# A retention-plus-Fourier-mixer kernel: the last batch pinned on every engine, its normalisation cut into separate pieces

## The chip, the cores and the metric

The kernel runs on one core of one Trainium2 chip. The metric is the device time of one execution in microseconds (us), lower is better. Three runs of the kernel before are given: 245.81, 246.08 and 246.43 us, median 246.08 us. One more execution was profiled; all durations in the prediction are from that one.

## The reference: what is computed

Two parts follow each other. The first is a recurrent retention layer with 4 batches, 8 heads, 768 steps and head size 64; the second takes its output as a tensor x of 4 x 768 x 512.

```python
for t in range(S):                       # retention, per batch and head
    state = gamma * state + outer(k[t], v[t])
    y[t] = scale * q[t] @ state
x = y, heads side by side                # (4, 768, 512)
u = x + real(fft(fft(x, axis=1), axis=2))
un = (u - mean(u)) / sqrt(var(u) + 1e-6) # over the 512 columns
out = u + relu(un @ w_ch1) @ w_ch2       # 512 -> 2048 -> 512
```

All inputs and the output are float32; the kernel multiplies in float16 and adds up in float32.

## The kernel before

Each batch is worked as 6 row blocks of 128 rows (index kb, 0 to 5). Four groups of work follow each other for a batch b: the retention (`attn_steps`, heads in pairs), the Fourier mixing of a row block (`s2_unit`: four matmuls L838, two copies on ScalarE L840/L841, two adds on VectorE L845/L848, two adds of x on GpSimd L875/L877), its normalisation (`norm_unit`, L895/L896 and after), its transposition (`unT_unit`; in the last batch a DMA transpose issued by SP, L938), and the two large matrix products. The matmuls of the products of batch b are the backbone, and the retention and the mixing of batch b+1 are sprinkled between them. `emit` sorts all units by a due time (b plus a fraction) and calls them in that order; the tile framework then schedules instructions on each engine by its own estimate, unless a manual dependency holds them. `pin` adds such dependencies: each instruction behind the one that stood before it on its engine. Before the change `pin` holds all engines only for the first batch's opening; up to time 1.0 it holds GpSimd; after that nothing.

The last batch (b = 3) differs from the others. Its products are made per pair of row blocks, p = 0, 1, 2. `h3_unit(p, n)`, n = 0 to 7, makes hidden blocks n and n+8 for the 256 rows of pair p: eight matmuls of 256 columns into one PSUM bank, tag `pm`, three banks in all (`ps_pm`). The bank is emptied with a ReLU into `ht16` by ScalarE (L1044) or by VectorE (L1046), as `H3_ACT` says: before the change VectorE has n = 2, ScalarE the other seven. Behind n = 3 and n = 7 VectorE makes four sums of `ht16` blocks each (L1063, called hsum here). `p3_unit(p, n)` then makes the seven products of a Strassen-like scheme (56 matmuls, L1103; 72 in pair 2, where two products go in column halves), and VectorE (L1096) and GpSimd (L1126) add them up; `wsum_unit` (L1024) has prepared sums of the second weight. The products of p = 0 follow in the order 1, 4, 2, 5, 6, 7, 3, and each row block's store goes out through SP (L1099).

Row blocks 0 to 2 of the last batch are mixed and normalised while the products of batch 2 still run; blocks 3, 4 and 5 while the last batch's own products run, at the due times `MIX3`: one tuple for each block, with times for mixing, `norm_unit`, `scaled_unit` and `unT_unit`. Pair p = 0 needs blocks 0 and 1 transposed, p = 1 blocks 2 and 3, p = 2 blocks 4 and 5. For the last batch the normalisation has these steps: statistics on VectorE (L895, L896), root on ScalarE (L898), reciprocal on VectorE (L912), a product mean times reciprocal on VectorE (L913), and on ScalarE the scaled rows `un` in float16 (L916). `un` has two buffers.

Batch 0's output rows are stored by `ch_unit` (L1004), one DMA of 128 x 512 float32 for each row block, on SP's queue, among the loads of later batches (L170) and the DMA transposes.

Of the kernel before, what the change touches and what calls it, by code (L numbers as in the profile page):

```python
# [11 lines left out]
AF = mybir.ActivationFunctionType  # L12
ALU = mybir.AluOpType
# [5 lines left out]
P = 128  # L19
B, H, S, D = 4, 8, 768, 64  # L20
DM = 512
# [15 lines left out]
LD0, LD1 = (0.172, 0.226), (-0.370, 0.140)  # L37
HT0 = (0.655, 0.675, 0.673, 0.628)
NPE = 2
MIX3 = ((0.005, 0.035, 0.070, 0.105), (0.190, 0.310, 0.325, 0.350), (0.355, 0.395, 0.420, 0.470))  # L40
WS = (0.7, 1.05)
H3_ACT = (0, 1, 3, 4, 5, 6, 7)
PROD = ((1, 4, 2, 5, 6, 7, 3), (1, 4, 6, 7, 5, 2, 3))
HS_AT = {3: (0, 4), 7: (4, 8)}
ACT_ROWS = ((2, 5, 6, 7, 8, 9, 10, 14), (0, 3, 6, 7, 9, 10, 11, 12, 14, 15))
# [3 lines left out]
def kernel(  # L49
# [9 lines left out]
    nc = tc.nc  # L59
# [36 lines left out]
    epsT = const.tile([P, 1], f32, tag="epsT")  # L96
# [10 lines left out]
    mark = [0]  # L107

    def pin(engines=None):
        ins = tc.nc.cur_bb.bb.instructions  # L110
        for n in range(mark[0], len(ins)):
            x = ins[n]
            e = str(x.engine)
            if engines is not None and not any(g in e for g in engines):
                continue
            if e in tails:
                tc.add_manual_dep(x, tails[e],
                                  mybir.DependencyInfo(mybir.DependencyClass.NoSync,
                                                       mybir.DependencyReason.DATA),
                                  reason="pinned order")  # L120
            tails[e] = x.name
        mark[0] = len(ins)
# [86 lines left out]
    for h in range(H):  # L209
# [6 lines left out]
                            op0=ALU.mult)  # L216
# [119 lines left out]
    for j in range(2):  # L336
        x = const.tile([P, NCH, 2, XW], f16, tag=f"x16_{j}", name=f"x16_{j}")
        xts.append(x)
        qz = const.tile([P, 2, NCH, P], f16, tag=f"q16z_{j}", name=f"q16z_{j}")
        qzs.append(qz)  # L340
        qt = const.tile([P, 2, NCH, P], f16, tag=f"qTz_{j}", name=f"qTz_{j}")
        qts.append(qt)
        t = const.tile([P, 257], f32, tag=f"qn_{j}", name=f"qn_{j}", padded_shape=[P, 260])
        nc.gpsimd.memset(t[:, 0:257:256], 0.0)
        qns.append(t)

    hid, nhid = xts[1][:, 0, 0, 0:P], xts[1][:, 0, 1, 0:P]
# [449 lines left out]
    lb = {}  # L797
# [85 lines left out]
    def norm_unit(b, kb):  # L883
        def run():
            u, stats = lb[b]["u"], lb[b]["st"]
            bst = stt.tile([P, 6], f32, tag=f"bst{kb % 3}", name="bst")
            un = up.tile([P, 2, 257], f16, tag="un16", name="un16").rearrange(
                "p a b -> p (a b)")[:, 0:DM]
            if b == 0 and kb < 3:
                for c0, c1 in (((0, 256), (256, DM)) if kb == 0 else ((0, DM),)):  # L890
                    una = nc.scalar.activation(un[:, c0:c1], u[:, kb, c0:c1], AF.Identity,
                                               bias=fd[0]["mu"][:, kb:kb + 1], scale=-1.0)
                lb[b]["bst", kb] = bst
            else:
                nc.vector.bn_stats(bst, u[:, kb, :])  # L895
                nc.vector.bn_aggr(stats[:, kb, 0:2], bst)  # L896
                if b == B - 1:
                    nc.scalar.activation(stats[:, kb, 2:3], stats[:, kb, 1:2], AF.Sqrt,  # L898
                                         bias=epsT, scale=1.0)
                    lb[b]["un", kb] = un  # L900
                    return
                una = nc.scalar.activation(un, u[:, kb, :], AF.Identity,  # L902
                                           bias=stats[:, kb, 0:1], scale=-1.0)
            lb[b]["un", kb] = un
            if b == 0 and kb == 2:
                lb[0]["una"] = una
        return run

    def scaled_unit(kb):
        def run():  # L910
            u, stats = lb[B - 1]["u"], lb[B - 1]["st"]
            nc.vector.reciprocal(out=stats[:, kb, 3:4], in_=stats[:, kb, 2:3])  # L912
            nc.vector.scalar_tensor_tensor(out=stats[:, kb, 2:3], in0=stats[:, kb, 0:1],  # L913
                                           scalar=-1.0, in1=stats[:, kb, 3:4], op0=ALU.mult,
                                           op1=ALU.mult)
            nc.scalar.activation(lb[B - 1]["un", kb], u[:, kb, :], AF.Identity,  # L916
                                 bias=stats[:, kb, 2:3], scale=stats[:, kb, 3:4])
        return run

    def rstd_unit(b, rt):  # L920
# [13 lines left out]
    def unT_unit(b, kb):  # L934
        def run():
            un, unT = lb[b].pop(("un", kb)), lb[b]["unT"]
            if b > 1 or b and kb >= 3:
                nc.sync.dma_start_transpose(unT[:, :, kb * P:(kb + 1) * P], un)  # L938
                return
            pst = ps_g.tile([P, 4, P], f16, tag="g", name="pst", padded_shape=[P, 8, P])  # L940
            for cb in range(4):
                nc.tensor.transpose(pst[:, cb, :], un[:, cb * P:(cb + 1) * P], ident16)
            if b == 0 and kb == 0:
                nc.scalar.copy(unT[:, 0:2, 0:P], pst[:, 0:2])
                nc.scalar.copy(unT[:, 2:4, 0:P], pst[:, 2:4])
            elif (kb % 2 == 0) != (b == 0 and kb < 3):
                nc.vector.tensor_copy(unT[:, :, kb * P:(kb + 1) * P], pst)
            else:
                nc.scalar.copy(unT[:, :, kb * P:(kb + 1) * P], pst)
        return run  # L950
# [39 lines left out]
    def ch_unit(b, rt, rb3, part):  # L990
        def run():
            rb = rt * 3 + rb3
            if part == 0:
                psc_of[0] = ps_pm.tile([P, DM], f32, tag="pm", name="psc")
            psc = psc_of[0]
            for fb in range(4 * part, 4 * part + 4):
                nc.tensor.matmul(psc, ht16[:, fb, rb3 * P:(rb3 + 1) * P], w216[:, fb, :],  # L997
                                 start=(fb == 0), stop=(fb == NFB - 1))
            if part == 3:
                ob = obp.tile([P, DM], f32, tag="ob", name="ob")  # L1000
                nc.vector.scalar_tensor_tensor(out=ob, in0=psc, scalar=lb[b]["st"][:, rb, 3:4],  # L1001
                                               in1=lb[b]["u"][:, rb, :], op0=ALU.mult,
                                               op1=ALU.add)
                nc.sync.dma_start(out[b, rb * P:(rb + 1) * P, :], ob)  # L1004
        return run

    def wsum_unit(j, hi):
# [58 lines left out]
    def p3_unit(p, n):  # L1066
        def run():
# [4 lines left out]
            end = p == 2  # L1072
# [40 lines left out]
            if n == 1:  # L1113
                nc.scalar.copy(w, ps)
            elif n == 2:
                add(o11, ps, u11)
                if end:
                    store(r0, 0, 256, o11)
            elif n == 4:
                add(u21, ps, u21)  # L1120
            elif n == 6:
                add(w, ps, w)
                if end:
                    add(u22, u22, w)
                for x in (u21, u12) if end else (u22, u21, u12):
                    nc.gpsimd.tensor_tensor(out=x, in0=x, in1=w, op=ALU.add)  # L1126
            elif n == 7:
                add(u22 if end else o22, ps, u22)
                add(o21, ps, u21)
                if end:  # L1130
                    store(r1, 0, 256, o21)
                else:
                    store(r1, 0, DM, o1)
# [105 lines left out]
    def mix_units(b, kbs):  # L1239
        s2s = [s2_unit(b, kb) for kb in kbs]  # L1240
        if b == B - 1:
            s2s = [u for kb, s2 in zip(kbs, s2s) for u in (s2, norm_unit(b, kb), scaled_unit(kb))]
        return s2s, [unT_unit(b, kb) for kb in kbs]

    def emit(streams):
        ev = []
        for si, (units, t0, t1) in enumerate(streams):
            for i, u in enumerate(units):
                ev.append((t0 + (t1 - t0) * (i + 1.0) / len(units), si, i, u))
        ev.sort(key=lambda e: e[:3])  # L1250
        for e in ev:
            e[3]()
            if e[0] < 1.0:
                behind()
                pin(None if e[0] < 0.05 else ["Pool", "GpSimd"])

    pin()
    for u in first_units():
# [7 lines left out]
    for b in range(B):  # L1266
# [19 lines left out]
        if b < B - 1:  # L1286
            s2s, unTs = mix_units(b, [3, 4, 5])
            dm = DM0 if b == 0 else DM1
            streams += [(s2s, b + dm[0], b + dm[1]), (unTs, b + dm[2], b + dm[3])]
        else:  # L1290
            for kb, due in zip((3, 4, 5), MIX3):
                streams += [([f], b + t, b + t) for t, f in zip(due, (
                    s2_unit(b, kb), norm_unit(b, kb), scaled_unit(kb), unT_unit(b, kb)))]
        if b + 1 < B:
            steps = attn_steps(b + 1)
            if b == 0:
# [51 lines left out]
```

## Time and profile before

| | us |
|---|---|
| median of three runs | 246.08 (245.81 to 246.43) |
| profiled execution, its own time | 245.54 |
| its span, first to last instruction | 243.8 |
| time around the span | 1.74 |
| TensorE busy in the span | 232.4 |
| VectorE / ScalarE / GpSimd busy | 191.1 / 130.9 / 87.2 |

In the profile PE is TensorE's matmuls, PEld its weight loads, DVE is VectorE, ACT ScalarE, POOL GpSimd, SP SyncE. A line number is that of the kernel before. "Idle before <- X" says that an engine sat idle and that X released it. Two instructions that follow each other on VectorE overlap a little: the next one starts up to 0.09 us before the end shown of the first. The granted TensorE clock was 0.999.

### The profile page before, as it was taken

The numbers are of one execution on the slowest core, as the hardware profiler recorded it, in microseconds if no ns is written. First come the engines' busy times: TensorE is split into PE (matmuls) and PEld (weight loads), VectorE is DVE, ScalarE is ACT, GpSimd is POOL, SyncE is SP. The second block draws the span as 40 slices with busy tenths as digits, with TensorE's granted clock in tenths as the row PEclk, the third lists the DMA queues.
The fourth block names the chain that finished last, engine by engine and source line by source line (L and its number), as shares of the span: only waits on it lengthen the run. The fifth ranks groups of instructions, "written<-read, shape, count | busy, mean of one in ns | idle before, by whom it ended". The sixth has DMA issues, their size and how long they took to land.

```text
span 243.8 us, 5673 instructions
## 1 busy us (share of the span) xinstructions
PE 232.4 (95%) x2160; PEld 156.3 (64%) x2160; DVE 191.1 (78%) x478; ACT 130.9 (54%) x286; POOL 87.2 (36%) x154
## 2 busy tenths in 40 slices
PE   6997899999999998999999999999999999989994
PEld 2454668956776655665567546565667469878883
DVE  8999957897897788996886778899996735775463
ACT  8798669588775434751247414741247527353340
POOL 6666601466600057690000545670002310430302
PEclk9999999999999999999999999999999999999999
DMA  8999999799999477999999467796200231031202
GB/s 174 255 261 143 197 197 205 175 249 246 282 222 225 74 170 167 196 191 133 263 270 216 106 127 207 141 116 145 87 2 1 45 126 46 3 109 24 86 3 86
DMA packets 99498, 36.41 MB, mean 149 GB/s; under 512 B 89872, under 2 KB 96656, under 8 KB 99472
## 3 DMA queue, kind: packets, MB, share of 16 engines
q1 hardware_dynamic: 95104, 31.79, 62.5%
q0 software_dynamic: 4224, 4.19, 10.7%
q8 instruction: 17, 0.28, 0.5%
q14 instruction: 9, 0.07, 0.1%
q10 hardware_dynamic: 144, 0.07, 0.1%
HBM read 27.26 MB, written 6.29 MB: 138 GB/s over the span
## 4 chain that ended last, share of the span: by engine, by line
PE 77%; DVE 6%; ACT 5%; SPq 4%; DMA 3%; issue 2%; POOL 1%; ACTq 0%; POOLq 0%
PE psc L997 25%; PE psh L958 19%; PE psc L1103 8%; PE psh L1039 7%; SPq L170 4%; PE wkA L605 3%; DMA q<-in_q_dram 3%; PE psh L975 3%; PE ps L741 3%; PE wkY L659 2%; PE pq L838 2%; PE wkY L655 1%; PE tq L561 1%; PE wkK L624 1%; ACT g L748 1%
## 5 line engine op out<-in xcount | busy, mean ns | idle before, releaser
L997 PE MATMUL psc<-w,ht 128*128 128x512 f16 x288 | 68.2, 379 | 0.0
L958 PE MATMUL psh<-unT,w 128*128 128x384 f16 x320 | 59.7, 326 | 0.0
L875 POOL TENSOR_TENSOR u<-u,x 128x256 f32<-128x256 f32 x21 | 13.4, 640 | 104.6 <-DVE u L845 95.2
L997 PEld LDWEIGHTS <-ht 128*128 128x128 f16 x288 | 27.2, 98 | 26.1 <-issue 0.2
L958 PEld LDWEIGHTS <-w 128*128 128x128 f16 x320 | 29.9, 98 | 15.8 <-issue 0.6
L962 ACT ACTIVATE ht<-psh 128x384 f16<-128x384 f32 x46 | 22.3, 490 | 23.6 <-PE psh L958 23.4
L608 DVE TENSOR_TENSOR atm<-wkA,maskp 128x512 f16<-128x512 f32 x36 | 23.8, 684 | 1.0 <-PE wkA L605 1.0
L1039 PE MATMUL psh<-unT,w 128*128 128x256 f16 x192 | 21.6, 272 | 0.6 <-DVE ht L1046 0.6
L1039 PEld LDWEIGHTS <-w 128*128 128x128 f16 x192 | 18.7, 98 | 2.9 <-issue 0.8
L964 DVE TENSOR_SCALAR ht<-psh 128x384 f16<-128x384 f32 x34 | 18.6, 549 | 1.8 <-PE psh L958 1.7
L895 DVE BATCH_NORM_STATS2 bst<-u 128x6 f32<-128x512 f32 x21 | 14.6, 695 | 6.6 <-POOL u L877 5.9
L634 DVE SCALAR_TENSOR_TENSOR s<-s,gk,wkK 128x128 f16<-128x128 f16 x48 | 16.5, 343 | 3.0 <-ACT s L630 2.2
L1001 DVE SCALAR_TENSOR_TENSOR ob<-psc,stats,u 128x512 f32<-128x512 f32 x18 | 13.4, 746 | 6.5 <-PE psc L997 6.5
L1044 ACT ACTIVATE ht<-psh 128x512 f16<-128x512 f32 x21 | 12.2, 594 | 10.2 <-PE psh L1039 10.1
L667 ACT ACTIVATE x<-wkY,gexp 128x384 f16<-128x384 f32 x24 | 12.8, 582 | 8.0 <-PE wkY L659 8.0
L902 ACT ACTIVATE un<-u,stats 128x512 f16<-128x512 f32 x15 | 10.8, 722 | 11.0 <-DVE stats L896 7.7
L156 PE MATMUL wps<-ht 128*128 128x512 f16 x40 | 13.5, 443 | 2.2 <-POOL ht L207 2.2
L388 POOL TENSOR_SCALAR kd<-k,gexp 128x384 f16<-128x384 f32 x24 | 13.9, 590 | 3.8 <-DMA k<-in_k_dram 3.8
L877 POOL TENSOR_TENSOR u<-u,x 128x256 f32<-128x256 f32 x21 | 13.3, 635 | 3.0 <-DVE stats L896 1.2
L605 PE MATMUL wkA<-qTz,kT 128*128 128x256 f16 x72 | 13.4, 273 | 0.1
L1126 POOL TENSOR_TENSOR u<-u,ws 128x256 f32<-128x256 f32 x8 | 5.8, 756 | 21.0 <-DVE ws L1096 18.9
L975 PE MATMUL psh<-unT,w 128*128 128x128 f16 x192 | 11.5, 219 | 0.1
(189 smaller groups left out, 424.0 us busy)
## 6 DMA issues: line engine op xcount, KB each, us to landing
q<-in_q_dram SPq DMA_DIRECT2D x16, 384.0 KB, 6.2
k<-in_k_dram SPq DMA_DIRECT2D x16, 384.0 KB, 5.5
v<-in_v_dram SPq DMA_DIRECT2D x16, 384.0 KB, 6.1
out_dram<-ob SPq DMA_DIRECT2D x22, 256.0 KB, 2.5
w<-in_moe_w_ch_dram POOLq DMA_DIRECT2D x8, 512.0 KB, 10.9
out_dram<-ob SPq DMA_DIRECT2D x3, 128.0 KB, 1.7
unT<-un SPq DMA_TRANSPOSE x15, 2.5
qTz<-q16z SPq DMA_TRANSPOSE x8, 3.9
```

Of the source, the lines that this page charges most:

```text
L388: kc = nc.gpsimd.tensor_scalar(out=kd[:, :, h2, :], in0=k32[:, h2], scalar1=gkd[:, h0 + h2:h0 + h2 + 1], scalar2=1.0, op0=ALU.mult, op1=AL ...
L605: mm = nc.tensor.matmul(wk[:, c2], st["kT"][:, c, :], st["qT"][:, :, c, :], start=True, stop=True)
L608: nc.vector.tensor_tensor(out=st["atm"][:, 2 * part:2 * part + 2], in0=wk, in1=maskp[:, PAIR_ORDER[i]].unsqueeze(1).to_broadcast([P, 2, 2, ...
L634: nc.vector.scalar_tensor_tensor(out=s16[:, c], in0=s16[:, c - 1], scalar=gk2[:, hp:hp + 1], in1=wk[:, c - c0], op0=ALU.mult, op1=ALU.add)
L895: nc.vector.bn_stats(bst, u[:, kb, :])
L958: nc.tensor.matmul(psh, w116[:, cb, fb * P:(fb + 1) * P], unT[:, cb, rt * 384:(rt + 1) * 384], start=(cb == 0), stop=(cb == 3))
L962: nc.scalar.activation(ht16[:, fb, :], psh, AF.Relu, bias=0.0, scale=-1.0)
L964: nc.vector.tensor_scalar(out=ht16[:, fb, :], in0=psh, scalar1=-1.0, scalar2=0.0, op0=ALU.mult, op1=ALU.max)
L975: mm = nc.tensor.matmul(psh[:, f], w116[:, cb, fb * P:(fb + 1) * P], unT[:, cb, kb * P:(kb + 1) * P], start=(cb == 0), stop=(cb == 3))
L997: nc.tensor.matmul(psc, ht16[:, fb, rb3 * P:(rb3 + 1) * P], w216[:, fb, :], start=(fb == 0), stop=(fb == NFB - 1))
L1039: nc.tensor.matmul(psh[:, t], w116[:, cb, fb * P:(fb + 1) * P], unT[:, cb, p * 256:(p + 1) * 256], start=(cb == 0), stop=(cb == 3))
L1103: nc.tensor.matmul(ps[:, c0:c1], lh(f), rh(f)[:, c0:c1], start=first and f == 0, stop=last and f == 7, skip_group_check=True)
```

## The change

- `emit` calls `pin()` for every event later than time 3, so the last batch's instructions keep the order in which they are written on all engines; the mark from which `pin` works is moved at each event.
- The last batch's normalisation has a piece more and a smaller one: `root_unit` (the root alone on ScalarE) is separate from `norm_unit`, with a due time of its own in `MIX3`, and `scaled_unit` makes `un` in one VectorE instruction, (u - mean) * reciprocal, in place of the small product on VectorE and the large one on ScalarE. All due times in `MIX3` are new.
- VectorE empties unit n = 4 of each pair in place of n = 2 (`H3_ACT`).
- The last batch's weight sums are due earlier (`WS`).
- Batch 0's stores are two DMAs of 256 columns for each row block.
- On GpSimd, two adds of the same operand for pairs 0 and 1 (u21 and u22) become one of 128 x 512 with the operand repeated; two small memsets at the start are gone.

```diff
-MIX3 = ((0.005, 0.035, 0.070, 0.105), (0.190, 0.310, 0.325, 0.350), (0.355, 0.395, 0.420, 0.470))
-WS = (0.7, 1.05)
-H3_ACT = (0, 1, 3, 4, 5, 6, 7)
+MIX3 = ((0.005, 0.085, 0.110, 0.125, 0.150), (0.190, 0.290, 0.310, 0.325, 0.350),
+        (0.345, 0.415, 0.435, 0.460, 0.500))
+WS = (0.6, 0.97)
+H3_ACT = (0, 1, 2, 3, 5, 6, 7)
...
-        nc.gpsimd.memset(t[:, 0:257:256], 0.0)
...
-                    nc.scalar.activation(stats[:, kb, 2:3], stats[:, kb, 1:2], AF.Sqrt,
-                                         bias=epsT, scale=1.0)
                     lb[b]["un", kb] = un
                     return
...
+    def root_unit(kb):
+        def run():
+            stats = lb[B - 1]["st"]
+            nc.scalar.activation(stats[:, kb, 2:3], stats[:, kb, 1:2], AF.Sqrt, bias=epsT,
+                                 scale=1.0)
+        return run
...
             nc.vector.reciprocal(out=stats[:, kb, 3:4], in_=stats[:, kb, 2:3])
-            nc.vector.scalar_tensor_tensor(out=stats[:, kb, 2:3], in0=stats[:, kb, 0:1],
-                                           scalar=-1.0, in1=stats[:, kb, 3:4], op0=ALU.mult,
-                                           op1=ALU.mult)
-            nc.scalar.activation(lb[B - 1]["un", kb], u[:, kb, :], AF.Identity,
-                                 bias=stats[:, kb, 2:3], scale=stats[:, kb, 3:4])
+            nc.vector.tensor_scalar(out=lb[B - 1]["un", kb], in0=u[:, kb, :],
+                                    scalar1=stats[:, kb, 0:1], scalar2=stats[:, kb, 3:4],
+                                    op0=ALU.subtract, op1=ALU.mult)
...
-                nc.sync.dma_start(out[b, rb * P:(rb + 1) * P, :], ob)
+                for c0, c1 in ((0, 256), (256, DM)) if b == 0 else ((0, DM),):
+                    nc.sync.dma_start(out[b, rb * P:(rb + 1) * P, c0:c1], ob[:, c0:c1])
...
                 if end:
                     add(u22, u22, w)
-                for x in (u21, u12) if end else (u22, u21, u12):
-                    nc.gpsimd.tensor_tensor(out=x, in0=x, in1=w, op=ALU.add)
+                    nc.gpsimd.tensor_tensor(out=u21, in0=u21, in1=w, op=ALU.add)
+                else:
+                    x = u[:, r1].rearrange("p (t m) -> p t m", t=2)
+                    nc.gpsimd.tensor_tensor(out=x, in0=x, in1=w.unsqueeze(1).to_broadcast(
+                        [P, 2, 256]), op=ALU.add)
+                nc.gpsimd.tensor_tensor(out=u12, in0=u12, in1=w, op=ALU.add)
...
             if e[0] < 1.0:
                 behind()
                 pin(None if e[0] < 0.05 else ["Pool", "GpSimd"])
+            elif e[0] > B - 1:
+                pin()
+            mark[0] = len(tc.nc.cur_bb.bb.instructions)
```

## The prediction

> **What bounds the kernel now.** I read the page first, then the busy times by stage, then the waits of TensorE, then the chain of work in the last batch. The page:
>
> ```profile
> span 243.8 us, 5673 instructions
> PE 232.4 (95%) x2160; PEld 156.3 (64%) x2160; DVE 191.1 (78%) x478; ACT 130.9 (54%) x286; POOL 87.2 (36%) x154
> ```
>
> TensorE's matmuls fill 95% of the span; the rest of that share can hide anywhere, so the stages matter. Columns: stage, its length, busy time by engine.
>
> ```profile
> 41.00:96.00 55.00, 54.09 (x554) 36.71 (x552) 45.80 (x117) 34.84 (x69) 21.72 (x34) 1.00 0.95 201
> 96.00:148.00 52.00, 52.00 (x413) 31.57 (x411) 42.08 (x99) 22.13 (x52) 18.83 (x32) 1.00 1.00 188
> 148.00:199.30 51.30, 51.00 (x406) 30.45 (x404) 41.98 (x104) 23.30 (x56) 15.99 (x27) 1.00 0.43 95
> 199.30:213.00 13.70, 13.70 (x133) 12.32 (x131) 9.36 (x27) 7.21 (x16) 3.43 (x6) 1.00 0.10 30
> 213.00:227.00 14.00, 13.38 (x123) 11.60 (x121) 8.66 (x23) 5.83 (x13) 3.60 (x6) 1.00 0.22 58
> 227.00:240.40 13.40, 13.34 (x137) 11.76 (x134) 7.83 (x22) 4.55 (x8) 2.64 (x4) 1.00 0.15 55
> ```
>
> The last three lines are the pairs p = 0, 1, 2 of the last batch, the only stage whose order the change pins. TensorE idles 0.00, 0.62 and 0.06 us there. Of the waits of this stage, only one has PE in front, and the chain shows what stands behind it:
>
> ```profile
> PE psh L1039 <- DVE ht L1046: 0.6, 1, 0.6
> ```
> ```profile
> 213.00 0.89 PE psh L1039 x8
> ...
> 213.97 0.61 ACT ht L1044
> 214.58 0.05 issue
> 214.63 0.49 DVE u L845
> 215.12 0.07 issue
> 215.19 0.64 POOL u L875
> 215.82 0.60 POOL u L877
> 216.43 0.02 issue
> 216.45 0.70 DVE bst L895
> 217.15 0.02 issue
> 217.18 0.18 DVE stats L896
> 217.36 0.58 DVE ht L1046
> 217.95 0.04 issue
> 217.99 2.78 PE psh L1039 x24
> ```
>
> In pair 1 VectorE's emptying of unit n = 2 stands in its queue behind row block 5's statistics, which wait for GpSimd. Unit n = 5 needs the bank of n = 2, so TensorE stops from 217.37 to 217.99. That is the only stall that this change can take away, and **0.62 us is the size of the prize**.
>
> **The change, part by part.**
>
> *TensorE's work.* The built programs (an order with its waits, no times) have the same TensorE stream instruction by instruction. What differs is which of the three banks each unit of the last batch takes and whom it waits for: up to batch 2 nothing, then units n = 3 to 7 of all pairs wait for ScalarE alone. The allocator no longer gives n = 5 or n = 7 the bank that VectorE empties late (n = 4's): n = 5 waits for n = 2 (ScalarE), n = 7 for n = 5 (ScalarE). Only the first product waits for VectorE's n = 4, at its fifth weight load.
>
> *Unit n = 2 moves to ScalarE, n = 4 to VectorE.* In pair 1 ScalarE empties n = 2 as soon as it is made, beside matmuls: the stall goes, **-0.62**. What is late next? ScalarE's eight commands per pair: a bank's unit takes 8 matmuls at 0.109 us (64 in 6.99), the emptying 0.60, so ScalarE keeps up. The tight place is n = 7 behind n = 5. From the last start of n = 5 to the first of n = 7 are nine starts, 0.98 us. Needed: 0.27 (one matmul) + 0.04 to 0.09 (lag of ScalarE behind the matmuls: n = 0 ended at 213.89 and L1044 began at 213.97) + 0.60 + 0.05 (217.94 to 217.99) = 0.96 to 1.01. So 0 to 0.03 for a pair; I take 0.02 each, **+0.06**.
>
> *VectorE's four sums now stand ahead of n = 4.* They need n = 3, which ScalarE ends 2.5 us before the next use; from 203.60 to 205.15 they took 1.55, n = 4 then 0.66: ready at 205.75 in pair 0. The first product's fifth weight load comes at about 206.84 (206.50 + 4 x 0.109, less 0.1): slack 1.1. Pair 2 the same, 0.8. No cost; were the cover gone, each us late is a us lost.
>
> *`un` on VectorE.* It removes L913 (0.19) and ScalarE's L916 (0.81), adds a 128x512 float32 VectorE instruction that no row shows. Bounds: 0.42 (L293, 386 columns of float32, median) and 0.75 (L1001, 512 columns, two tensors); I take 0.67 (L1046, same operation and columns, out of PSUM). Blocks 0 to 2: before, ScalarE began block 1's `un` at 192.35 and SP's transposes at 191.47; the statistics row set these times, the new ones follow within 0.3. A transpose lands 2.4 us after its issue, so blocks 0 and 1 are there by 196, needed at 199.44: 3 us of cover. `un` of block 2 reuses block 0's buffer and now VectorE does that wait; behind it stands only a store's add that is ready at 195.7. Free.
>
> *Block 5's chain in pair 0 and 1, the one place without much cover.* Products 5, 6 and 7 start at 209.12, so 6 ends at 209.12 + 15 x 0.109 + 0.27 = 211.03, VectorE's add to w (0.42) at 211.5; the GpSimd add of 128x512: between 0.73 (as one of L1126) and 1.38 (two by their spacing of 0.69); I take 1.38 as it reads as much: 212.9. Then two adds (0.7), reciprocal (0.16), `un` of block 4 (0.67), the o12 add (0.34): L845 of block 5 starts at 214.8, against 214.63 before. The rest as before, 2.73 to the end of L896: 217.5 instead of 217.36. Behind it ScalarE's root, 0.29, ahead of unit n = 5 in ScalarE's queue, which TensorE has ready at 218.24: slack 0.4. VectorE's sums and n = 4 follow, ready at 219.7, needed at 220.3. No cost; with the low prices 0.9 us of room.
>
> *The transposes of blocks 3 to 5.* Block 4's now stands behind two stores on SP: issued near 215.5, landed 218, needed at 226.3. Block 3: `un` ends at 206.6, landed 209.2, needed at 212.84. Block 5: 220.5, 223, needed at 226.3. Free.
>
> *Batch 0's stores in halves.* Six more issues on SP at 0.36 to 0.49 each (86.27, 95.94). Behind the first three: loads of batch 2, cast only from 91.61 on, 20 us later. Behind the later ones: transposes at 92.63 and 98.09 that wait for GpSimd's casts after SP had idled 0.6 and 1.2 us. Cost 0; the kT of batch 2 that lands at 97.3 is used by TensorE at 99.15, 1.8 us of cover.
>
> *The rest.* Weight sums: in the built order only one small reciprocal moves, 0. Two memsets less (0.16 us at 3.87): the GpSimd cast behind them starts earlier, but the next waits 1.04 us for a load, and the chain of the start goes through SP's issues to 11.69 and a load of 7.67: 0, at most -0.16.
>
> **Sum:** -0.62 + 0.06 = -0.56 us: span 243.2, the profiled execution 245.54 -> 245.0. That execution was 0.54 below the median of 246.08; the same shift on the median gives **245.5 us** (-0.23%). About 0.3%, 0.74 us, is what a measurement of this kernel can tell from no change, so the forecast is: no difference that can be told.
>
> **The rivals.**
>
> 1. *Given back.* The 0.62 goes, but two-bank rotation costs 0.15 to 0.2 in each pair instead of 0.02 (ScalarE empties with only 0.02 us to spare). For: 0.96 to 1.01 against 0.98. Against: the weight loads wait of 0.26 for unit 7 is all that ScalarE cost TensorE so far. 0.62 - 0.6 = 0: 246.0.
> 2. *Slower: the root blocks ScalarE in pair 1.* If VectorE and GpSimd hinder each other, L896 of block 5 ends late, the root behind it holds ScalarE's queue, and n = 5 is not emptied. It costs from 0.4 us of lateness on, and is a net loss from 0.4 + 0.62 - 0.06 = about 1.0; with 2.3 late (an `un` of 1.5 instead of 0.67, the two GpSimd adds doubled, +2.1) it is +0.8 slower: 247.3. For: one L1126 took 0.968 beside VectorE's add of two SBUF operands at 237.36, seven others 0.72. Against: 0.24 is all that the trace shows.
> The Trainium skill (GPSIMD Engine Reference, Key points) says that GpSimd shares its SBUF interfaces with VectorE and that they collide when VectorE runs in a two-port mode or reads two SBUF inputs; the 0.968 agrees. It speaks against `un` on VectorE beside GpSimd's adds: by it one collision of 0.24 in this chain leaves 0.2 of the slack, and the time stays 245.5.
> The Trainium skill (VectorE: DVE Perf Modes, The perf-mode tier table) lets a float32 tensor_scalar in SBUF run at twice the rate; its cost formula gives an estimate of 0.33 us for `un`, by which the chain is 0.3 earlier and the sum the same; no row here shows it.
> 3. *Slower: SP's queue.* A half store delays a transpose by more than its cover of 1.8 us. Six halves cost 2.7 at most, if all idle time of SP were gone: +0.9, 247.0.
> 4. *More than the stall.* The start gains 0.16, and the 0.17 us slips of the first product in pairs 1 and 2 (its eight matmuls took 1.20, in pair 0 1.03) vanish: 0.62 + 0.5 = 1.1: 245.0. Against the slips: they are unit 7's emptying, which stays.
>
> **How the numbers follow.** Forecast (gain 0.4 to 0.74) 0.46; rival 1 0.22; rival 4 0.22; rival 2 0.06; rival 3 0.04. Faster by over 0.3% (below 245.34): rival 4 and a little of the forecast's spread, since three runs lie 0.6 apart: 0.27. Slower by over 0.3%: rivals 2 and 3, 0.10. Within: 0.63. The range goes from rival 4's 245.0 less the runs' 0.1 to rival 1's 246.0 plus their 0.35: 244.9 to 246.4, which leaves out rivals 2, 3 and the tails.
>
> **What would show it.** In the profile after, no wait of PE for DVE ht in the last batch; TensorE idle under 0.1 us in each pair; n = 7 starting at most 0.05 us after n = 5's emptying; L896 of block 5 ending before 217.9 on the old clock; the `un` row on VectorE between 0.42 and 0.75. I am wrong if PE waits for ScalarE or a DMA in the last batch, if `un` takes over 1 us, or if a stage before 188 us changes its length by over 0.3.

## The result, and the profile after

The kernel after takes 245.70 us (median of 20 runs, 245.11 to 246.07), the kernel before beside it 246.31 us (20 runs, 245.81 to 246.98): a ratio of 0.9972 with a 95% interval of 0.9963 to 0.9980, or -0.61 us. That is a gain, and the interval lies wholly below 1, but it is smaller than the 0.3% that the prediction set as the least that it would call a difference. The forecast was 245.5 us and -0.56 us. The 0.2 us between 245.5 and 245.70 stems from the starting point: the three runs that the forecast started from had a median of 246.08, the twenty of 246.31.

The profiled execution of the kernel after took 245.43 us; that of the kernel before 245.54. First the page of the kernel after:

```profile
span 243.4 us, 5668 instructions
PE 231.2 (95%) x2160; PEld 155.6 (64%) x2160; DVE 192.5 (79%) x478; ACT 126.7 (52%) x280; POOL 87.7 (36%) x150
```

With `un` moved, ScalarE is busy 4.2 us less than before and VectorE 1.4 more; neither is the bound. Next the busy time by stage of the last batch (columns: stretch, its length, then busy time of PE, PEld, DVE, ACT, POOL, the clock, the DMA share, GB/s):

```profile
199.30:213.00 13.70, 13.70 (x130) 12.16 (x128) 9.84 (x24) 5.58 (x14) 3.29 (x5) 1.00 0.10 30
213.00:227.00 14.00, 14.00 (x131) 12.30 (x130) 9.13 (x25) 5.54 (x12) 3.67 (x6) 1.00 0.20 58
227.00:240.40 13.40, 13.15 (x135) 11.56 (x132) 8.11 (x22) 4.55 (x8) 2.30 (x3) 1.00 0.17 59
```

In the middle one TensorE was busy for 13.38 us before and fills all 14.00 now. The 0.25 missing from the third lies behind the last product. The list of TensorE's waits in this stage, one line long before, is empty now. The chain of work (start, duration, what):

```profile
199.98 6.99 PE psh L1043 x64
...
207.20 6.11 PE psc L1107 x56
...
213.54 7.02 PE psh L1043 x64
220.56 6.27 PE psc L1107 x56
226.83 7.01 PE psh L1043 x64
233.84 6.33 PE psc L1107 x72
...
240.19 0.29 DVE ob L1100
```

(L1043 is the L1039 of before, L1107 its L1103, L1048 and L1050 the emptyings L1044 and L1046.) The chain holds nothing but TensorE until the last add (the lines left out are block 4's and 5's mixing, 0.23 us each, and an issue). In pair 1 the 64 products of h3 take 7.02 us; before they took 220.77 - 213.00 = 7.77. I call **the last batch's length** the time from the first product of h3 in pair 0 to the start of the last VectorE add: 240.38 - 199.44 = 40.94 before, 240.19 - 199.98 = 40.21 now, a gain of 0.73.

The span fell by 0.4 only, because this execution came to the last batch 0.54 later (199.98 against 199.44). Up to 41 us the two agree; by 62 us it is 0.44 late, because TensorE waited 0.40 for GpSimd's work on a load of k in batch 1 that landed later. That load was issued before the first of the halved stores (61.34); another 0.10 comes between 146 and 160 us. The time of the issue isn't the reason: it was 54.17 here and 53.83 in the kernel before, but the kernel before with halved stores (in the table below) issues this load at 53.60 and waits 0.39, and the run with narrow adds at 54.08 and doesn't wait. In the profiled executions of ten kernels that work in the same way until then, but for small things in the mixing (this one and nine below), h3 of pair 0 began between 199.47 and 199.98, with a median of 199.56. In the three without halved stores it began between 199.34 and 199.56, in the kernel before with halved stores at 200.05. So most of the 0.54 is that one execution. Whether the opening is some 0.1 us longer can't be told from these.

### The profile page after: what moved, and what is told of

Same layout as the page of the kernel before. It is cut to its first block, busy times and chain, and to the rows that moved or that the text cites. A ratio compares the mean times of both kernels' runs of the same rounds, so it can differ in the third digit from the quotient of the medians.

```text
span 243.4 us, 5668 instructions
## 1 busy us (share of the span) xinstructions
PE 231.2 (95%) x2160; PEld 155.6 (64%) x2160; DVE 192.5 (79%) x478; ACT 126.7 (52%) x280; POOL 87.7 (36%) x150
## 4 chain that ended last, share of the span: by engine, by line
PE 71%; DMA 7%; ACT 7%; DVE 6%; SPq 4%; POOL 2%; issue 2%; ACTq 0%; POOLq 0%; DVEq 0%
PE psc L1000 21%; PE psh L961 19%; PE psh L1043 9%; PE psc L1107 8%; DMA k<-in_k_dram 5%; SPq L171 4%; PE wkA L605 3%; PE ps L741 3%; DMA q<-in_q_dram 2%; PE wkY L659 2%; PE pq L838 2%; PE wkY L655 1%; ACT un L891 1%; PE wkK L624 1%; DVE bst L895 1%
## 5 line engine op out<-in xcount | busy, mean ns | idle before, releaser
L875 POOL TENSOR_TENSOR u<-u,x 128x256 f32<-128x256 f32 x21 | 13.4, 637 | 105.6 <-DVE u L845 97.4
L1043 PE MATMUL psh<-unT,w 128*128 128x256 f16 x192 | 21.5, 273 | 0.0
L1043 PEld LDWEIGHTS <-w 128*128 128x128 f16 x192 | 18.7, 98 | 2.2
L1048 ACT ACTIVATE ht<-psh 128x512 f16<-128x512 f32 x21 | 12.5, 597 | 13.6 <-PE psh L1043 7.9
L900 ACT ACTIVATE un<-u,stats 128x512 f16<-128x512 f32 x15 | 10.8, 722 | 12.1 <-DVE stats L896 7.9
L157 PE MATMUL wps<-ht 128*128 128x512 f16 x40 | 12.6, 418 | 2.2 <-POOL ht L208 2.2
L877 POOL TENSOR_TENSOR u<-u,x 128x256 f32<-128x256 f32 x21 | 13.5, 644 | 3.0 <-DVE stats L896 3.0
L840 ACT COPY qn<-pq 128x128 f32<-128x128 f32 x18 | 4.9, 273 | 14.2 <-PE pq L838 14.2
```

The lines of the kernel that those rows point to most:

```text
L877: nc.gpsimd.tensor_tensor(out=u[:, kb, 256:512], in0=u[:, kb, 256:512], in1=x[:, kb, 1, 257:1:-1], op=ALU.add)
L1043: nc.tensor.matmul(psh[:, t], w116[:, cb, fb * P:(fb + 1) * P], unT[:, cb, p * 256:(p + 1) * 256], start=(cb == 0), stop=(cb == 3))
```

## The experiments

Theory A: what the change gains is the one stop of TensorE, and whether TensorE stops in the last batch is decided by what stands in a queue ahead of the emptying of a unit of h3: the root and `un` on ScalarE, the statistics on VectorE. Rivals: B, the pin as such is what gains; C, the choice of the unit that VectorE empties (and so the banks) is; D, something else in the change (the stores, fewer GpSimd operations). The runs in one table; "runs" is the difference of the medians from the kernel before beside it:

| kernel | last batch, us | against 40.94 | runs, us | ratio, 95% interval |
|---|---|---|---|---|
| after | 40.21 | -0.73 | -0.61 | 0.9963 to 0.9980 |
| before + pin | 43.89 | +2.95 | +2.99 | 1.0113 to 1.0149 |
| before + n = 4 on VectorE | 42.10 | +1.16 | +0.84 | 1.0026 to 1.0051 |
| after, without the pin | 42.18 | +1.24 | +1.02 | 1.0037 to 1.0063 |
| after, `un` on ScalarE | 43.54 | +2.60 | +2.79 | 1.0092 to 1.0133 |
| after, n = 2 on VectorE | 40.16 | -0.78 | -1.02 | 0.9951 to 0.9978 |
| before + halved stores | 40.95 | +0.01 | +0.10 | 0.9984 to 1.0007 |
| after, narrow GpSimd adds | 40.21 | -0.73 | -0.59 | 0.9960 to 0.9983 |
| after, root with statistics | 40.28 | -0.66 | -0.40 | 0.9975 to 0.9997 |
| after, block 5 late by one | 40.21 | -0.73 | -0.49 (one run) | |
| after, block 5 late by three | 41.52 | +0.58 | +0.64 (one run) | |
| after, n = 7 in halves | 39.89 | -1.05 | -0.83 | 0.9945 to 0.9977 |
| after, n = 7 in halves, n = 2 on VectorE | 39.84 | -1.10 | -1.09 | 0.9939 to 0.9971 |

In every row the last batch's length accounts for the runs within 0.33 us, in seven of thirteen within 0.2.

### The pin alone

```diff
+            elif e[0] > B - 1:
+                pin()
+            mark[0] = len(tc.nc.cur_bb.bb.instructions)
```

> The kernel before with the pin of the last batch added and nothing else (its own due times, unit 2 on VectorE, un on ScalarE). Theory A, the gain comes from where the root, un and the emptying of unit 2 stand in their queues, and the pin only fixes what is written: written order puts block 3's root behind unit 0 and un behind unit 1 on ScalarE, so in pair 0 unit 4 waits for a bank some 0.9 us, and in pair 1 unit 6 waits another 0.7 behind un: 1.5 us slower than before, 0.6%. Rival B, pinning as such takes the stall away: 0.6 to 0.75 faster than before.

Measured: 248.95 us, +2.99. TensorE's waits and parts of the chain:

```profile
PE psh L1039 <- ACT ht L1044: 2.0, 2, 1.3
PE psh L1039 <- DVE ht L1046: 1.0, 1, 1.0
```
```profile
201.05 1.32 POOL u L877
...
203.34 0.29 ACT stats L898
203.63 0.49 ACT ht L1044
...
204.17 3.73 PE psh L1039 x32
...
215.42 0.04 ACT un L916
...
216.60 0.50 DVE u L845
...
219.34 0.59 DVE ht L1046
...
219.97 1.05 PE psh L1039 x8
```

Pair 0: the root of block 3 is written with its statistics, so the pin puts it ahead of n = 1 on ScalarE; n = 1 waits from its products' end at about 201.2 until 203.63, and n = 4, which takes its bank, stands for 1.3 us. Pair 1: `un` of block 4 stands ahead of block 5's copies on ScalarE, so block 5's add L845 begins at 216.60 (214.63 in the kernel before) and the statistics hold VectorE's n = 2 until 219.34. The other 0.7 us of waiting for ScalarE, at n = 6, is the one that I had expected behind `un` of block 5. Rival B falls: a pin of an order that was written for a scheduler costs 3 us, about twice what I expected, because I had missed the second delay, by way of the copies (and one GpSimd add of block 3 took 1.32 us instead of 0.60, the first line of the chain; the last section comes back to it).

The pin alone also takes hold of something that I hadn't thought of. With the old `WS` the last two weight sums are due after time 3, up to 2 + 1.05, so the pin puts them into pair 0 (L1024 at 200.64 and 203.22), where VectorE's 1.22 us at 200.64 stand beside that slow GpSimd add. In the kernel before, the scheduler started the last of them at 169.47. The new `WS` ends at 2 + 0.97, outside the pinned part, and in the kernel after the last one starts at 170.02. So the earlier weight sums, which the prediction put at 0, seem to be a part that the pin needs; no run changes them alone, so their worth stays open.

### The unit on VectorE alone

```diff
-H3_ACT = (0, 1, 3, 4, 5, 6, 7)
+H3_ACT = (0, 1, 2, 3, 5, 6, 7)
```

> The kernel before with VectorE emptying unit 4 in place of unit 2 and nothing else. Theory A: ScalarE now has unit 2, and its queue still holds block 5's root, which waits for VectorE's statistics, ahead of it: the stall in pair 1 grows from 0.6 to about 1.5 us, and pair 0 gets one of 0.7 (unit 6 behind un): about 1.6 us slower than before, 0.65%. Rival C, the choice of the unit on VectorE is what takes the stall away: 0.6 to 0.75 faster than before, no TensorE wait in pair 1.

Measured: 246.80 us, +0.84. Waits, and the chain in pair 1:

```profile
PE psh L1039 <- ACT ht L1044: 1.4, 3, 0.9
```
```profile
217.70 0.19 DVE stats L896
...
218.12 0.59 ACT ht L1044
...
218.78 0.04 ACT un L916
...
219.50 0.59 ACT ht L1044
...
220.12 1.91 PE psh L1039 x16
```

VectorE is no longer waited for, but ScalarE has the same wait for block 5's statistics in front of it, now as the root, and `un` too. Rival C falls as far as the unit by itself is concerned: the new unit costs time without the pin and the new pieces. The size was about half of what I had expected by the runs, and 1.16 of 1.6 us by the last batch.

### After, with n = 2 on VectorE

```diff
-H3_ACT = (0, 1, 2, 3, 5, 6, 7)
+H3_ACT = (0, 1, 3, 4, 5, 6, 7)
```

> The kernel after with unit 2 on VectorE again, all else kept (pin, due times, un on VectorE). Theory A: in the written order the emptying of unit 2 stands ahead of block 5's statistics, done near 217.0 where unit 5 needs it at 217.9 on this kernel's clock, so no stall: same as after within 0.1 us, TensorE idle in pair 1 under 0.1. Rival C: the stall of 0.6 to 0.75 us comes back, as slow as before.

Measured: 244.94 us, 0.9964 of before; TensorE waits for nothing in the last batch, and h3 takes the same 6.99 in all pairs (the second and third are shown):

```profile
213.27 6.99 PE psh L1043 x64
...
226.53 6.99 PE psh L1043 x64
```

VectorE's queue in pair 1 (start, duration, instruction) shows why the stop is gone even with the old unit:

```profile
215.93 0.69 DVE L1050 TENSOR_SCALAR ht<-psh 128x512 f16<-128x512 f32 x1 [0.20 <-PE psh L1043]
216.68 0.69 DVE L895 BATCH_NORM_STATS2 bst<-u 128x6 f32<-128x512 f32 x1
```

The written order has the emptying ahead of the statistics; in the kernel before it stood behind them. With the order pinned, the choice of unit is worth 0.05 us, and in favour of the old one: it takes away the 0.03 and 0.02 us by which h3 of pairs 1 and 2 is longer in the kernel after. By the runs alone the two kernels can't be told apart, since their intervals overlap.

### After without the pin

```diff
-            elif e[0] > B - 1:
-                pin()
-            mark[0] = len(tc.nc.cur_bb.bb.instructions)
```

> The kernel after without the pin, all else kept. Theory A: the scheduler moves block 5's root ahead of unit 2 on ScalarE (stall of about 1.0 in pair 1) and unit 7 gets the bank that VectorE empties behind un and three sums (0.65 in pairs 0 and 1): about 2.3 us slower than after, 0.9%, and 1.6 slower than before. Rival C: 0.6 to 0.75 faster than before, as after. Rival D, the gain has another source than the last batch (stores, start): same as after.

Measured: 246.98 us, +1.02, where +1.6 was expected. The waits and the chain of pair 1:

```profile
PE psh L1043 <- ACT ht L1048: 0.9, 1, 0.9
PE psh L1043 <- DVE ht L1050: 0.6, 2, 0.3
```
```profile
217.83 0.19 DVE stats L896
...
218.04 0.02 ACT stats L910
...
218.25 1.07 ACT ht L1048 x2
...
219.34 1.09 DVE hsum L1067 x3
220.44 0.61 DVE ht L1050
...
221.09 1.03 PE psh L1043 x8
```

The scheduler puts the root ahead of n = 2 and n = 3 on ScalarE; n = 2, 3, the four sums and VectorE's n = 4 are late one after the other, and n = 7 has been given the bank that VectorE empties. So the new pieces and times need the pin, and the pin needs them.

### After, with `un` on ScalarE again

```diff
-            nc.vector.tensor_scalar(out=lb[B - 1]["un", kb], in0=u[:, kb, :],
-                                    scalar1=stats[:, kb, 0:1], scalar2=stats[:, kb, 3:4],
-                                    op0=ALU.subtract, op1=ALU.mult)
+            nc.vector.scalar_tensor_tensor(out=stats[:, kb, 2:3], in0=stats[:, kb, 0:1],
+                                           scalar=-1.0, in1=stats[:, kb, 3:4], op0=ALU.mult,
+                                           op1=ALU.mult)
+            nc.scalar.activation(lb[B - 1]["un", kb], u[:, kb, :], AF.Identity,
+                                 bias=stats[:, kb, 2:3], scale=stats[:, kb, 3:4])
```

> The kernel after, still pinned, but `un` of blocks 0 to 5 of the last batch is made by ScalarE again, with the small VectorE product ahead of it (0.19 us) and ScalarE's 0.81 in place of VectorE's 0.54. Theory A (what matters is what stands ahead of a unit's emptying in a pinned queue): in pairs 0 and 1 ScalarE's queue then holds root, `un`, units n = 5, 6, 7, and `un` waits for VectorE's reciprocal and product behind the root. In pair 1 L896 ends at 217.87, so root to 218.20, reciprocal and product to about 218.6, `un` 218.6 to 219.4, n = 5 to 220.0, against the 218.24 on the clock of before (218.78 on that of after) at which it is ready: a stop of 0.4 to 0.7 at n = 7 and about 0.6 to 1.2 more at the first product, which needs units 5 to 7. The same in pair 0. Together +2 to +3.6 us against the kernel after, about 248.5, +0.9% against the kernel before, with PE waiting for ScalarE's emptying (L1048's line) in pairs 0 and 1. Rival B (the pin alone, or the units' banks, is what gained; the engine of `un` is only a matter of taste): as the kernel after, 245.7 +- 0.2, no such wait.

Measured: 248.56 us, +2.79 against before; the last batch is 43.54 - 40.21 = 3.33 longer than in the kernel after, inside the expected +2 to +3.6. TensorE's two largest waits, then ScalarE's queue in pair 1:

```profile
PE psc L1109 <- ACT ht L1050: 1.0, 5, 0.2
PE psh L1045 <- DVE ht L1052: 0.9, 2, 0.7
```
```profile
219.44 0.29 ACT L910 ACTIVATE stats<-stats,epsT 128x1 f32<-128x1 f32 x1 [0.53 <-DVE stats L896]
221.88 0.81 ACT L921 ACTIVATE un<-u,stats 128x512 f16<-128x512 f32 x1 [2.15 <-DVE stats L918]
222.60 1.55 ACT L1050 ACTIVATE ht<-psh 128x512 f16<-128x512 f32 x3
```

The path is not the one I wrote: I let `un` follow the root at 218.6, but its small VectorE product (L918) stands in VectorE's queue behind the four sums and n = 4, so ScalarE idles 2.15 us with n = 5, 6 and 7 behind `un`, and the first product waits for them. Before that, TensorE stands 0.7 us ahead of n = 7 for VectorE's n = 4, which I hadn't foreseen: `un` of block 4 holds block 5's copies on ScalarE, as in the run with the pin alone, so block 5's statistics end 5.03 us after the first product of h3 instead of 4.33, and the sums and n = 4 behind them are late. Of the parts that were taken back one at a time, moving `un` to VectorE, where it stands behind what it waits for and holds no emptying on ScalarE, is worth the most: 3.33 us of the last batch, against 1.97 for the pin. The new due times in `MIX3` were not taken back by themselves.

### The halved stores alone, and the GpSimd adds

```diff
-                nc.sync.dma_start(out[b, rb * P:(rb + 1) * P, :], ob)
+                for c0, c1 in ((0, 256), (256, DM)) if b == 0 else ((0, DM),):
+                    nc.sync.dma_start(out[b, rb * P:(rb + 1) * P, c0:c1], ob[:, c0:c1])
```

> The kernel before with only the stores of batch 0 halved. Theory A: SP has 0.6 and 1.2 us of idle time and the transposes 1.8 us of cover: 0 +- 0.1 us, the same as before, and the wait of PE for VectorE's n = 2 (0.6) still there. Rival 3 of the prediction (six more issues delay a transpose): +0.2 to +0.9 us, and PE or ScalarE waiting for a DMA between 86 and 105 us. Rival D (the halved stores gave part of the gain): -0.1 to -0.3 us.

Measured: 245.87 against 245.77 us, a ratio of 0.9995 (0.9984 to 1.0007), and TensorE's one wait is the old one (L1040 and L1047 are the kernel before's L1039 and L1046):

```profile
PE psh L1040 <- DVE ht L1047: 0.6, 1, 0.6
```

Then the kernel after with the wide GpSimd add as two narrow ones:

```diff
-                    x = u[:, r1].rearrange("p (t m) -> p t m", t=2)
-                    nc.gpsimd.tensor_tensor(out=x, in0=x, in1=w.unsqueeze(1).to_broadcast(
-                        [P, 2, 256]), op=ALU.add)
+                    nc.gpsimd.tensor_tensor(out=u22, in0=u22, in1=w, op=ALU.add)
+                    nc.gpsimd.tensor_tensor(out=u21, in0=u21, in1=w, op=ALU.add)
```

> The kernel after with the wide GpSimd add (128x512, 1.27) made as two of 128x256 again (about 0.69 from one to the next, so 1.38). Theory A: block 5's chain in pair 1 is about 0.1 later inside a cover of about 0.8: the same time as the kernel after, +-0.1 us, no wait of PE in the last batch. Rival (fewer GpSimd operations give a part of the gain): +0.1 us or more against the kernel after.

Measured: 245.03 us, 0.9971, against 0.9972 of the kernel after; the last batch 40.21 in both, without a wait. Rival D falls for these two parts. The two memsets that are gone and the earlier weight sums were not tried by themselves.

### How much cover block 5 has

One and three GpSimd operations that multiply by 1.0 are put between block 5's adds and its statistics:

```diff
+                if b == B - 1 and kb == 5:
+                    for _ in range(3):
+                        nc.gpsimd.tensor_scalar(out=u[:, kb, :], in0=u[:, kb, :], scalar1=1.0,
+                                                scalar2=1.0, op0=ALU.mult, op1=ALU.mult)
                 nc.vector.bn_stats(bst, u[:, kb, :])
```

> The kernel after with three GpSimd multiplications of block 5's 128x512 by 1.0 put between its two adds (L875, L877) and its statistics (L895): block 5's chain is late by three of them. Nearest rows: 0.59 for 128x384 and 0.93 for 128x768 of GpSimd's tensor_scalar, so 0.65 to 0.75 each, 1.95 to 2.25 late. Theory A (the prediction's rival 2 as a mechanism: the root stands ahead of n = 5 in ScalarE's queue and has 0.68 us of cover by the trace after): TensorE stops in pair 1 at n = 7, for 1.95 - 0.68 to 2.25 - 0.68 = 1.3 to 1.6 us, with 0.1 for filling the pipe, and the span is 1.4 to 1.7 longer than the kernel after's (about 244.8 to 245.1). PE's wait is for ScalarE's emptying, not for VectorE. Rival (the cover is larger than the slack to n = 5, since the bank of n = 5 is needed only by n = 7): stop below 0.7. Rival (units behind the statistics on VectorE, the four sums and n = 4, are what decides): PE waits for VectorE's n = 4 at the first product instead.

> The kernel after with one GpSimd multiplication of block 5's 128x512 by 1.0 (0.63 long, 0.70 from one to the next in the run with three) between its two adds and its statistics: L896 about 0.70 late. The run with three was 2.11 late and lost 1.30 in pair 1, so the cover is about 0.8 (0.68 of ScalarE's idle time ahead of n = 5, and 0.1 to 0.2 between its emptying and n = 7). Theory A: 0.70 is inside the cover: TensorE stops for no more than 0.1, the products of h3 of pair 1 take 7.0 to 7.15 and the last batch 40.2 to 40.35. Rival (lost time grows evenly with lateness): 1.30 x 0.70 / 2.11 = 0.43, pair 1's h3 7.45.

Three: the statistics (L900 here) end at 219.50, which is 2.10 later than in the kernel after if both are counted from h3 of pair 0. ScalarE's emptyings are L1052 here:

```profile
PE psh L1047 <- ACT ht L1052: 1.2, 1, 1.2
```
```profile
219.31 0.19 DVE stats L900
...
219.73 0.58 ACT ht L1052
...
220.36 1.03 PE psh L1047 x8
221.39 6.27 PE psc L1111 x56
```

TensorE stands before n = 7 and waits for n = 5 behind the root, nothing else; h3 of pair 1 takes 221.39 - 213.07 = 8.32 instead of 7.02, so 2.10 late costs 1.30, and 0.8 is covered if each us beyond the cover costs a us. One: 0.71 late, h3 of pair 1 takes 7.02 and the last batch 40.21, as in the kernel after. Lost time doesn't grow with the delay from zero: an even growth would have made 0.71 cost 0.44. By these two runs the cover lies above 0.71, at about 0.8 us.

### The root with the statistics

```diff
-                streams += [([f], b + t, b + t) for t, f in zip(due, (
-                    s2_unit(b, kb), norm_unit(b, kb), root_unit(kb), scaled_unit(kb),
-                    unT_unit(b, kb)))]
+                streams += [([f], b + t, b + t) for t, f in zip(due[:2] + due[3:], (
+                    s2_unit(b, kb), norm_root(b, kb), scaled_unit(kb), unT_unit(b, kb)))]
```

(`norm_root` calls `norm_unit` and `root_unit`.)

> The kernel after, with the square root written with the statistics again (one piece, as in the kernel before) instead of in a piece of its own. In the built order of ScalarE it then stands one place earlier in pairs 0 and 1: ahead of the emptying of n = 3 instead of behind it; nothing else moves. Theory A (only what stands ahead of an emptying matters): pair 0, root from 203.28, when n = 3 is not ready until 203.51: nothing. Pair 1: L896 of block 5 ends at 217.87, so n = 3, ready at 217.13, is emptied from 218.15 to 218.75, 1.0 later; n = 6 needs its bank at 218.78: 0 to 0.05 lost; VectorE's four sums need n = 3 and n = 4 stands behind them, so n = 4 ends at about 220.9 instead of 219.92 and the first product needs it at 220.74: 0.1 to 0.3 lost. Together +0.1 to +0.4 against the kernel after, about -0.15% against the kernel before. Rival (the pin and `un` on VectorE are all that counts, the separate root is worth nothing): as the kernel after, +-0.05, last batch 40.2 long. Rival (n = 3 late holds n = 6 and all behind it): +0.7 or more.

Measured: 245.22 us, 0.9986 (0.9975 to 0.9997). ScalarE in pair 1:

```profile
217.48 0.29 ACT L910 ACTIVATE stats<-stats,epsT 128x1 f32<-128x1 f32 x1 [1.05 <-DVE stats L896]
217.68 0.58 ACT L1054 ACTIVATE ht<-psh 128x512 f16<-128x512 f32 x1
```

n = 3 is late as expected, and h3 of pair 1 takes 7.10 us instead of 7.02; the first product is not late (its piece of the chain is 6.27 as before), so VectorE's n = 4, ready at 220.44 here, was still in time. The last batch is 0.07 longer, just below the expected 0.1 to 0.4. Its median is 0.19 above that of the kernel with narrow adds, run beside it, but the intervals of the two overlap: by the trace the separate root is worth 0.07 us, and more than that isn't shown.

### n = 7 in halves, and both better variants together

```diff
-            if n in H3_ACT:
+            if n == 7:
+                nc.scalar.activation(ht16[:, 7, 0:256], psh[:, 0], AF.Relu, bias=0.0, scale=1.0)
+                nc.vector.tensor_scalar(out=ht16[:, 15, 0:256], in0=psh[:, 1], scalar1=1.0,
+                                        scalar2=0.0, op0=ALU.mult, op1=ALU.max)
+            elif n in H3_ACT:
```

> The kernel after with unit n = 7 of the last batch emptied in halves, one 128x256 by ScalarE and the other by VectorE at the same time. Theory A: in pairs 1 and 2 the first product loses 0.17 us each (its eight matmuls take 1.20 instead of 1.03) because its weights wait for ScalarE's emptying of unit 7 (0.60 to 0.65 for 256 columns of two halves); in halves this is over 0.2 to 0.3 us earlier, so both slips go: -0.3 us against the kernel after, 245.4, about -0.37% against the kernel before. Rival: a VectorE instruction more per pair stands behind the four sums and unit 4 (pair 1: unit 4 ends at 219.92, the new one at about 220.3, needed at the last weight load of the first product, about 221.1), if VectorE is late the first product waits for it instead and the time is as in the kernel after or up to 0.5 us longer.

Measured: 244.94 us, 0.9961 of before. TensorE's first product of pair 1, first in the kernel after, then here:

```profile
220.40 1.20 PE L1107 MATMUL psc<-w,ht 128*128 128x256 f16 x8
```
```profile
219.89 1.04 PE L1111 MATMUL psc<-w,ht 128*128 128x256 f16 x8
```

The slip of 0.16 in the first product is gone in pairs 1 and 2: 40.21 - 39.89 = 0.32, as expected. Then both:

> The kernel after with unit n = 7 in halves (one by ScalarE, the other by VectorE) and unit n = 2 on VectorE, n = 4 on ScalarE, as the kernel before had it: the two variants that were faster than the kernel after, together. Theory A: there is no stop left that either could remove twice: the last batch 39.8 to 40.0 (39.89 with the halves alone, 40.15 with n = 2 alone), about -0.35% against the kernel before, the same as the halves alone. Rival (n = 2 on VectorE saved something of its own, 0.05): 39.83. Rival (VectorE's n = 2 stands behind block 5's statistics again and TensorE stops in pair 1): 40.3 or more.

Measured: 244.53 us, 0.9955 (0.9939 to 0.9971), the lowest median of this case, though the interval overlaps those of the two variants alone. Pair 1 of its chain:

```profile
213.13 6.99 PE psh L1043 x64
220.12 6.11 PE psc L1111 x56
```

Both numbers are the least that any pair showed. The last batch is 39.84 us, so the 0.32 of the halves and the 0.05 of n = 2 add up.

## Why the prediction was right, and where its terms were off

- **The stop of 0.62 us.** The mechanism was right: it went, and nothing took its place. Its price was too low. TensorE's 24 products behind it took 2.78 us, where 24 at the pace of 0.109 take 2.62. The line was in the chain that I showed. A product is shown 0.27 us long but the next starts 0.11 after it, so the idle time begins 0.16 later than the time lost does. The stop cost 0.62 + 0.16 = 0.78 us; h3 of pair 1 fell by 0.75, and two-bank rotation took 0.03.
- **Two-bank rotation, 0.06.** Measured 0, 0.03 and 0.02 in the three pairs, 0.05 in all. The run with n = 2 on VectorE has 6.99 in all three, so it is the unit's choice that costs it.
- **`un` on VectorE, taken at 0.67, bounds 0.42 and 0.75.** Measured 0.54. The Trainium skill (VectorE: DVE Perf Modes, The perf-mode tier table) gave, by the page's cost formula and the table's doubled rate, an estimate of 0.33 us; the trace has 0.54, above it and below the 0.68 of VectorE's operation on as many columns out of PSUM (L1050). The lower bound of 0.42 was misread: it is the median of five L293 of two widths, and the three of 386 columns have a mean of 0.44.
- **The wide GpSimd add, taken at 1.38.** Measured 1.27, with 0.73 for the other; worth nothing either way.
- **Block 5's cover, 0.4.** L896 ended at 217.87, which is 217.33 on the clock of before, not 217.5, and ScalarE idled 0.68 ahead of n = 5. The two late runs put the cover at about 0.8. Rival 2 of the prediction is right as a mechanism, and its point of beginning was too low by half; 0.17 of the difference is that the statistics came earlier than I let them.
- **Stores, sums, transposes, memsets: 0.** Stores and adds are shown by their runs; the sums ahead of n = 4 and the transposes only by the absence of a wait. The weight sums cost 0 in this change, but the reason that I gave (only a reciprocal moves) leaves out that their old times would have put two of them into the pinned part.
- **The sum.** -0.56 was said; the last batch fell by 0.73 and the runs by 0.61. Rival 4 (also the slips of the first product) did not come about in this change, rightly: they are the emptying of unit 7, and the run with that unit in halves removed them. Rival 1 (given back by rotation) was 0.05. The 0.3% that I took for the least that can be told was too wide for twenty runs of each kernel: their interval of 0.9963 to 0.9980 tells a gain of 0.2 to 0.4%.
- **Sums of rivals that don't come out.** Rival 2 counts a net loss from about 1.0 late, so 2.3 late would be 1.3 slower, 247.4; its +0.8 fits neither that nor its own 247.3. Rival 3's 247.0 leaves out the gain of 0.56 that would still be there; with it the time is 246.4, at the upper end of the range instead of outside it. Neither changes the forecast.
- **What I said would make it wrong.** A stage before 188 us did change by over 0.3, in the one profiled execution. The nine others with the same opening don't show it, so that bound was narrower than what one execution can tell.
- **What the prediction did not say.** It treated the parts as a sum of small terms. The runs show that they are not: the pin without the new pieces is +2.99, the new pieces without the pin +1.02, the new unit alone +0.84, the pin with `un` on ScalarE +2.79, all together -0.61.

## What to carry to other kernels

A stop of TensorE cost more here than the idle time shown (0.78 us for 0.62): compare the length of the piece of work that holds it with the same piece without it. Before pinning a written order, walk each queue and ask of every instruction that waits what stands behind it: here a `un` of 0.81 us on ScalarE, which waits for VectorE, turned a gain of 0.6 us into a loss of 2.8. And measure cover by delaying: here a delay of 0.71 us was free, and one of 2.10 cost 1.30.

## What was not expected of the hardware

In the run with the pin alone, one GpSimd add of 128x256 took 1.35 us; the same line takes 0.64 as a rule. Beside it VectorE worked on an addition of two SBUF operands:

```profile
200.64 1.22 DVE L1024 TENSOR_TENSOR wsum<-w,wsum 128x1536 f16<-128x1536 f16 x1
```
```profile
200.41 0.64 POOL L875 TENSOR_TENSOR u<-u,x 128x256 f32<-128x256 f32 x1 [8.27 <-DVE u L845]
201.01 1.35 POOL L877 TENSOR_TENSOR u<-u,x 128x256 f32<-128x256 f32 x1
```

L877 ends 0.50 us after L1024 does, so it seems to have stood still until about then: 0.7 us lost, three times the 0.24 that I had taken as the largest collision, and a term of the 1.3 us for which TensorE stands in pair 0 of that run. L1024, which began while L875 ran, took 1.22 us where this form takes 0.95 in the kernel before. The Trainium skill (SBUF — State Buffer, SBUF: two separate sides) says that VectorE with two SBUF inputs and a reading GpSimd take the shared ports as a lock, and that the one that comes second is blocked for the whole instruction; this run agrees with its 0.7 us. `un` itself met one GpSimd add in the kernel after (L877 at 192.61, 0.82 us instead of 0.64), in a stage where TensorE didn't wait for it; that add, too, ends 0.50 us after the VectorE instruction does (192.93).
